# First batch and first run in plain float32 products instead of three split passes

## The chip, the cores and the metric

The kernel runs on one NeuronCore of a Trainium2 chip. The metric is the device time of one execution in microseconds; times are medians over runs, and one further execution is profiled. The engines are named as in the profile: PE (TensorE's matmuls), PEld (its weight loads), DVE (VectorE), ACT (ScalarE), POOL (GpSimd) and SP (SyncE, which issues the DMAs).

## The reference

```python
# q, k, v: (8, 8, 576, 64) float32; w_in (512, 2048), w_out (2048, 512), both float64
k_p = k.reshape(B, H, 72, 8, D).mean(axis=3)          # pooled over 8 positions
v_p = v.reshape(B, H, 72, 8, D).mean(axis=3)
scores = q @ k_p.T / sqrt(D)
attn = softmax(scores)                                # sum + 1e-9
x = (attn @ v_p) -> (B * S, H * D) = (4608, 512)
h = x @ w_in
out = np.maximum(0.01 * h, h) @ w_out                 # (4608, 512) float32
```

The first part is attention against pooled keys and values, the second a two-layer block with a leaky ReLU between the layers. The weights arrive as float64 and are handled as pairs of 32-bit words.

## The kernel before

**Split products.** Most products of the kernel are made in three passes. An operand is held as two float32r tiles: `hi`, its rounded copy (a cast on ACT), and `lo`, the remainder (a subtraction on DVE). A product is then hi x hi + hi x lo + lo x hi, three matmuls that accumulate in one PSUM tile. The score product (L394) alone is a plain float32 matmul.

**Attention.** The eight batches are cut into tiles of 128 or 64 query rows, and neighbouring tiles form pieces of at most 320 rows. The units of a batch have short names: `lk`, `lv` pool k and v; `ku`, `vu` put them in place (`vu` makes `v_hi`, `v_lo` and `v_rem`); `q` transposes a query tile; `sa` makes scores, maximum and exponentials (the sums come with them); `sb` normalises into `at`; `pu` transposes `at` into `pT_hi`, `pT_lo` and `pT_rem`; `au` multiplies by v (L468 to L471) and writes the x tiles `xh` and `xl` of the next layer (L479, L480), or the last 64 rows of batches 0 and 1 into `x_tail`. A tile has two halves g = 0, 1 (four heads each), so `sa31` is tile 3, half 1; a piece too, so `au10` is piece 1, half 0. The last 8 of the 72 pooled positions (`rem`) are held apart.

**Weights.** Both layers are cut into 16 slices f. `stage(f)` has SP load the words of slice f; a conversion consists of a head (two ACT and three DVE instructions, L184 to L190, which make one float32 tile) and a tail (L194 on ACT, L195 on DVE, which make its hi and lo). The steps are issued in a fixed sequence; `c` in the string `FIRST`, and `convert_to(n)` in the main loop, issue the next of them. In the program a conversion's head stands ahead of what follows it; which instruction runs first on ACT, DVE and POOL is decided by a planner from its own costs. PE's order is the program's (manual_schedule).

**Runs.** x is cut into nine chunks of 512 rows. A part is one chunk with one slice f. `m1` computes h for a part (12 matmuls L651 to L653 in two halves, then leaky ReLU L656, cast L659 and subtraction L660 into `gh`, `gl`); `m2` adds its share to the output (12 matmuls L675 to L677), two parts later. Run 0 is chunk 0 with f = 0 to 7, run 1 chunk 1 with all f, run 2 chunk 0 with f = 8 to 15, and so on, one chunk each. The output of run 0 is kept in DRAM as `partial` and added in run 2. The units of the attention that the next chunks need are spread between the halves of m1 and m2: after batch 0's units (the string `FIRST`), run 0 carries the end of batch 0 (`TAIL_STEPS`) and all of batch 1.

**Space.** Weights, the raw k and v of the first batches and other passing tiles share places by tag: `spare(f, i, ...)` is the place of slice f of layer i.

## Time and profile before

| | |
|---|---|
| median of 3 runs | 1011.18 us (1011.02 to 1089.97) |
| profiled execution | 1009.92 us, span of its instructions 1008.1 us |
| granted TensorE clock over the span | 0.978 |
| busy share of PE, PEld | 95%, 78% |
| busy share of DVE, ACT, POOL | 36%, 42%, 18% |
| DMA | 57.44 MB, mean 57 GB/s |

The shares are means over the whole span. The stretch that the change touches is the first 134 us, and there they are quite different; the prediction shows them by stretch. In the rows of the timeline an instruction stands with its start, its duration, engine, line, operation, tiles and count; in brackets the idle time before it and what ended it.

### The profile page before, as it was taken

To read this page: it belongs to the slowest core of one execution; us is meant where nothing else is said; L and a number is where in the kernel's file an instruction comes from. 1 tells how busy PE (TensorE), PEld (TensorE's weight loads), DVE (VectorE), ACT (ScalarE), POOL (GpSimd) and SP (SyncE) were. 2 spreads that over 40 slices of the span, in tenths; PEclk is the share of its full clock that TensorE was granted. 3 is DMA by queue.
4 is the path that set the end of the run, shared out by engine and by line. 5 is a ranking of instruction groups with operands and counts; after the bars stand their busy time and mean duration, and the time that the engine had idled before them with its cause. 6 is when DMAs were issued, how large, how long until landed. Compare 5 with 4: busy or idle time off the path is not lost.

```text
span 1008.1 us, 12812 instructions
## 1 busy us (share of the span) xinstructions
PE 960.3 (95%) x4584; PEld 785.7 (78%) x4584; DVE 366.3 (36%) x890; ACT 427.4 (42%) x1386; POOL 177.7 (18%) x292
## 2 busy tenths in 40 slices
PE   4569999999999999999999999999999999999998
PEld 4457778888887878878888788888887788888886
DVE  5998639223333222232222323232322322231111
ACT  4778657234433333434343425333434334332221
POOL 3602200501036510141013301031100001000000
PEclk8689999999999999999999999999999999999999
DMA  9954311302034301130012202020200020001001
GB/s 241 279 172 133 101 46 44 112 23 69 1 107 115 91 8 44 32 92 12 20 44 58 58 11 63 3 61 1 63 11 11 1 63 1 1 1 42 1 1 42
DMA packets 65006, 57.44 MB, mean 57 GB/s; under 512 B 39856, under 2 KB 48048, under 8 KB 64944
## 3 DMA queue, kind: packets, MB, share of 16 engines
q1 hardware_dynamic: 64944, 56.64, 19.8%
q8 instruction: 36, 0.59, 0.2%
q14 instruction: 26, 0.21, 0.1%
HBM read 46.14 MB, written 10.49 MB: 56 GB/s over the span
## 4 chain that ended last, share of the span: by engine, by line
PE 89%; DVE 4%; ACT 3%; issue 1%; DMA 1%; SPq 0%; POOL 0%; DVEq 0%; ACTq 0%; POOLq 0%
PE ph L651 13%; PE acc L675 13%; PE ph L653 13%; PE ph L652 13%; PE acc L677 13%; PE acc L676 13%; PE pss L394 4%; PE pp L443 2%; PE pq L369 2%; ACT e L404 2%; PE pa L468 1%; PE pa L469 1%; PE pa L471 1%; PE pa L470 1%; DVE w_t L187 1%
## 5 line engine op out<-in xcount | busy, mean ns | idle before, releaser
L651 PE MATMUL ph<-xh,w 128*128 128x512 f32 x576 | 236.2, 410 | 0.0
L675 PE MATMUL acc<-w,gh 128*128 128x512 f32 x576 | 234.7, 408 | 0.0
L653 PE MATMUL ph<-xh,w 128*128 128x512 f32 x576 | 227.2, 394 | 0.0
L652 PE MATMUL ph<-xl,w 128*128 128x512 f32 x576 | 227.0, 394 | 0.0
L677 PE MATMUL acc<-w,gl 128*128 128x512 f32 x576 | 225.7, 392 | 0.0
L676 PE MATMUL acc<-w,gh 128*128 128x512 f32 x576 | 225.5, 392 | 0.0
L656 ACT ACTIVATE ph<-ph 128x512 f32<-128x512 f32 x144 | 84.2, 585 | 275.6 <-PE ph L653 275.4
L660 DVE TENSOR_TENSOR gl<-ph,gh 128x512 fp32r<-128x512 f32 x144 | 99.4, 691 | 264.9 <-ACT gh L659 264.0
L418 POOL TENSOR_TENSOR at<-e,red 128x256 f32<-128x256 f32 (+1 forms) x76 | 47.3, 622 | 561.8 <-DVE red L416 428.0
L404 ACT ACTIVATE e<-pss,red 128x72 f32<-128x72 f32 (+1 forms) x320 | 98.0, 321 | 108.8 <-DVE red L402 107.3
L653 PEld LDWEIGHTS ph<-xh,w 128*128 128x128 f32 x576 | 109.3, 190 | 24.4
L677 PEld LDWEIGHTS acc<-w,gl 128*128 128x128 f32 x576 | 108.4, 188 | 24.1
L651 PEld LDWEIGHTS ph<-xh,w 128*128 128x128 f32 x576 | 109.4, 190 | 22.2 <-issue 1.4
L675 PEld LDWEIGHTS acc<-w,gh 128*128 128x128 f32 x576 | 108.4, 188 | 21.9 <-issue 1.9
L652 PEld LDWEIGHTS ph<-xl,w 128*128 128x128 f32 x576 | 109.6, 190 | 19.4
L676 PEld LDWEIGHTS acc<-w,gh 128*128 128x128 f32 x576 | 108.6, 189 | 19.2
L659 ACT CAST gh<-ph 128x512 fp32r<-128x512 f32 x144 | 85.2, 592 | 3.1
L402 DVE TENSOR_REDUCE red<-pss 128x4 f32<-128x288 f32 (+1 forms) x80 | 36.1, 454 | 99.6 <-PE pss L394 98.5
L404 ACT ACTIVATION_READ_ACCUMULATOR e<-pss,red 128x1 f32 (+1 forms) x320 | 65.8, 206 | 0.0
L394 PEld LDWEIGHTS pss<-kT,qT 128*128 128x128 f32 (+1 forms) x320 | 49.4, 192 | 14.7 <-ACT qT L371 5.0
L394 PE MATMUL pss<-kT,qT 128*128 128x144 f32 (+1 forms) x320 | 55.9, 303 | 4.2 <-ACT qT L371 4.2
L449 DVE TENSOR_TENSOR pT_lo<-pp,pT_hi 128x256 fp32r<-128x256 f32 (+1 forms) x80 | 31.6, 395 | 69.5 <-ACT pT_rem L446 68.7
(90 smaller groups left out, 857.3 us busy)
## 6 DMA issues: line engine op xcount, KB each, us to landing
out_dram<-o SPq DMA_DIRECT2D x35, 256.0 KB, 2.1
q<-in_q_dram SPq DMA_DIRECT2D x32, 256.0 KB, 4.2
w_bits<-in_moe_w_in_dram SPq DMA_DIRECT2D x16, 512.0 KB, 3.6
w_bits<-in_moe_w_out_dram SPq DMA_DIRECT2D x16, 512.0 KB, 3.4
k0raw<-in_k_dram SPq DMA_DIRECT2D x16, 256.0 KB, 3.7
k1raw<-in_k_dram SPq DMA_DIRECT2D x16, 256.0 KB, 4.4
v0raw<-in_v_dram SPq DMA_DIRECT2D x16, 256.0 KB, 4.2
v1raw<-in_v_dram SPq DMA_DIRECT2D x16, 256.0 KB, 5.4
```

The lines of the kernel that those rows point to most:

```text
L394: nc.tensor.matmul(sc[:n, 2 * SP * i : 2 * SP * (i + 1)], qT[:, p, :n], kT[:, p, :, :].rearrange("d i s -> d (i s)"), start=True, stop=True,)
L404: ins = nc.scalar.activation(e[:n, h, :], scv[:n, h, :], AF.Exp, bias=mx[:n, h : h + 1], accum_out=sm[:n, h : h + 1],)
L418: eng.tensor_tensor(at[:n, 0:2, :].rearrange("a i (h s) -> a (i h) s", h=2), e[:n, :, 0:MAIN], sm[:n].unsqueeze(2).broadcast_to([n, 4, MAI ...
L651: nc.tensor.matmul(ph, w[:, 0, ks], xh[kk], start=kk == 0, stop=False)
L652: nc.tensor.matmul(ph, w[:, 0, ks], xl[kk], start=False, stop=False)
L653: nc.tensor.matmul(ph, w[:, 1, ks], xh[kk], start=False, stop=kk == NK - 1)
L656: nc.scalar.activation(ph, ph, AF.Prelu, alpha=0.01)
L659: casts.append(nc.scalar.copy(gh, ph))
L660: nc.vector.tensor_tensor(gl, ph, gh.bitcast(F32), op=ALU.subtract)
L675: nc.tensor.matmul(a, gh[:, r], hi, start=first, stop=False)
L676: nc.tensor.matmul(a, gh[:, r], lo, start=False, stop=False)
L677: nc.tensor.matmul(a, gl[:, r], hi, start=False, stop=last)
```

## The change

For batch 0 the values are kept as one float32 tile `v_first`, and `pT` as one float32 tile (its two main blocks copied by ACT, the remainder block multiplied by the mask `m_lo` on DVE); `au` makes two plain float32 matmuls where there were four. For chunk 0 in run 0, x is one float32 tile (`whole_x`), the weights of slices 0 to 7 stay in the float32 tile that the head makes (`whole_w`), the leaky ReLU writes one float32 tile `g`, and m1 and m2 are one plain float32 matmul per product instead of three split ones. The tails of slices 0 to 7 leave the sequence of steps and are issued when the slice's m2 of run 0 has been issued; `split_first` makes hi and lo of chunk 0's x in the second part of run 1, for run 2. Staging of slice f + 4 is issued behind the head instead of the tail. `FIRST` has 8 conversion steps, all heads, where it had 14 heads and tails, and some tiles lie in other places.

```diff
@@ FIRST
-        "lk ku q0 q1 sa00 sb00 sa01 sb01 lv sa10 sb10 sa11 sb11 q2 sa20 sa21 vu pu00 pu10 c c q3 "
-        "pu01 pu11 c sb20 sb21 au00 sa30 sa31 c au01 c pu20 pu21 sb30 sb31 c c pu30 pu31 c au10 au11 "
-        "c q4 c c / sa40 sa41 sb40 sb41 c c c"
+        "lk ku q0 q1 sa00 sb00 sa01 sb01 lv sa10 sb10 sa11 sb11 q2 sa20 sa21 vu pu00 pu10 c q3 "
+        "pu01 pu11 sb20 sb21 c au00 sa30 sa31 au01 c pu20 pu21 sb30 sb31 c pu30 pu31 c au10 au11 "
+        "q4 c / c sa40 sa41 sb40 sb41 c"
...
+    v_first = wts.tile([P, NK, 2, D], F32, tag="w1_8", name="v_first")
+    nc.gpsimd.memset(v_first, 0.0)
...
+    WHOLE_W = {0: (1, 0), 1: (2, 0), 2: (3, 0), 3: (6, 0), 4: (6, 1), 5: (7, 0), 6: (7, 1)}
+    whole_w = {}
+    def whole_weights(f):
+        if f not in whole_w:
+            shape, name = [P, 2, DM], f"whole{f}"
+            whole_w[f] = (
+                spare(*WHOLE_W[f], shape, F32, name) if f in WHOLE_W
+                else two.tile(shape, F32, tag="raw", name=name)
+            )
+        return whole_w[f]
@@ convert, head
-            ws[i, f] = spare(f, i, [P, 2, DM], F32R, f"w{i}_{f}")
-            t = five.tile([P, DM], I32, tag="o", name=f"w{i}_t{f}")
-            st["w"] = t.bitcast(F32)
+            if f < SPLIT:
+                t = whole_weights(f)[:, i, :]
+                st["w"] = t
+                t = t.bitcast(I32)
+            else:
+                t = five.tile([P, DM], I32, tag="o", name=f"w{i}_t{f}")
+                st["w"] = t.bitcast(F32)
...
+            if i == 1:
+                stage(f + SPARE)
@@ convert, tail
-            w, t = ws[i, f], st["w"]
+            w, t = spare(f, i, [P, 2, DM], F32R, f"w{i}_{f}"), st["w"]
+            ws[i, f] = w
             nc.scalar.copy(w[:, 0, :], t)
             nc.vector.tensor_tensor(w[:, 1, :], t, w[:, 0, :].bitcast(F32), op=ALU.subtract)
-            if i == 1:
-                stage(f + SPARE)
@@ place_v
+            if b == 0:
+                nc.scalar.mul(v_first[r, :, i, :], sums[r], 1.0 / POOL)
+                continue
@@ p_unit
+        if b == 0:
+            anchor["act"] = nc.scalar.copy(pc["hi"][:, :, o : o + n], pp[:, 0:2, :n])
+            nc.vector.tensor_scalar_mul(rem, pp[:, 2, :n], m_lo)
+            return
@@ av_unit
+            if b == 0:
+                vw = v_first[:, p, :, :].rearrange("a i d -> a (i d)")
+                nc.tensor.matmul(pa, vw, pc["hi"][:, i, :w], start=True, stop=False)
+                nc.tensor.matmul(pa, vr.bitcast(F32), pc["rem"][:, :w], start=False, stop=True)
...
-            if m:
+            if m and c == 0:
+                (nc.vector.tensor_copy if i else nc.scalar.copy)(whole_x(p)[:, o : o + m], pa[:, :m])
+            elif m:
...
+    def split_first():
+        for kk, (h, l) in enumerate(zip(*x_parts(0))):
+            nc.scalar.copy(h, whole_x(kk))
+            nc.vector.tensor_tensor(l, whole_x(kk), h.bitcast(F32), op=ALU.subtract)
@@ m1
+        if n == 0:
+            for kk in range(NK):
+                ks = slice(kk * P, (kk + 1) * P)
+                nc.tensor.matmul(
+                    ph, whole_w[f][:, 0, ks], whole_x(kk), start=kk == 0, stop=kk == NK - 1
+                )
+                if kk == 1:
+                    yield
+            g = three.tile([P, CH], F32, tag="gh", name=f"g{nm}")
+            casts.append(nc.scalar.activation(g, ph, AF.Prelu, alpha=0.01))
+            gs[k] = g, None
+            yield
+            return
@@ m2
+            if n == 0:
+                nc.tensor.matmul(a, gh[:, r], whole_w[f][:, 1, :], start=first, stop=last)
@@ steps
+        if f < SPLIT:
+            splits[i, f] = tail
+            continue
@@ main loop
             if n == 0:
-                convert_to(14 + 2.8 * f)
+                convert_to(min(8 + 2 * (f + 1), 2 * SPLIT) + 2 * max(0, f - 3))
             elif n == 1:
-                convert_to(36 + 3 * f)
+                convert_to(2 * SPLIT + 8 + 3 * (f + 1))
+                if f == 1:
+                    split_first()
...
             at += 1
+            for i in range(2):
+                if (i, at - 3) in splits:
+                    splits[i, at - 3]()
```

## The prediction

> **What bounds the kernel now.** First the windows view, cut where the program changes: until 52 us batch 0's attention runs alone, from 52 to 134 us the first run (chunk 0 with f 0 to 7, batch 1's attention beside it), from 134 us the second run. Columns: stretch, length, busy time and instructions of PE, PEld, DVE, ACT and POOL, granted clock, DMA share, GB/s.

> ```profile
> 27.00:52.00 25.00, 12.82 (x64) 10.65 (x64) 25.00 (x51) 16.65 (x53) 16.00 (x18) 0.66 1.00 287
> 52.00:83.00 31.00, 22.72 (x96) 17.71 (x96) 27.84 (x62) 24.91 (x68) 3.85 (x6) 0.83 0.57 171
> 83.00:134.00 51.00, 44.91 (x229) 35.50 (x228) 33.67 (x88) 36.65 (x133) 9.94 (x18) 0.97 0.29 87
> 134.00:220.00 86.00, 86.00 (x381) 71.12 (x380) 42.09 (x79) 40.08 (x76) 13.73 (x18) 1.00 0.21 65
> ```

> From 134 us PE has no idle time, so whatever the change does must show as an earlier or later start of that dense part. DVE is busy 25.00 us of 25 before 52 us and 27.84 of 31 after it; from 83 us PE is nearer to its limit (44.91 of 51) than DVE (33.67). So there are two regimes: DVE sets the pace up to about 83 us, PE after it. The second view is what PE waited for between 27 and 134 us (total, times, longest):

> ```profile
> PE pa L469 <- DVE pT_lo L449: 7.4, 4, 4.5
> PE pp L443 <- DVE at L418: 5.0, 2, 4.3
> PE pp L443 <- DVE x_tail L482: 3.1, 2, 1.8
> PE pp L443 <- POOL at L418: 2.9, 1, 2.9
> PE pq L369 <- ACT e L404: 2.6, 2, 2.1
> PE pq L369 <- DVE kT L330: 2.4, 1, 2.4
> PE pv L357 <- DVE v_rem L360: 0.5, 1, 0.5
> ```

> Three quarters of it end on DVE. Third, PE's timeline with the points where the stretches begin: the first product of the first run (51.94), the fourth m1 (83.12) and the first product of the second run (133.94).

> ```profile
> 51.94 0.50 PE L651 MATMUL ph<-xh,w 128*128 128x512 f32 x1
> ...
> 83.12 0.39 PE L651 MATMUL ph<-xh,w 128*128 128x512 f32 x1
> ...
> 133.94 0.39 PE L651 MATMUL ph<-xh,w 128*128 128x512 f32 x1
> ```

> PE's order is written by hand: 51.94 to 83.12 holds m1 of parts 0 to 2 and m2 of part 0 (16 products of 128x128 by 512), 83.12 to 133.94 holds m1 of 3 to 7 and m2 of 1 to 5 (40), and m2 of parts 6 and 7 (8 products) come after it.

> **The price of a whole product.** A split product is three matmuls. The only plain float32 matmul of before is the score product L394, 144 columns wide.

> ```profile
> L394 PE MATMUL pss<-kT,qT 128*128 128x144 f32 (+1 forms) x320 | 55.9, 303 | 4.2 <-ACT qT L371 4.2
> ...
> 92.57 0.39 PE L653 MATMUL ph<-xh,w 128*128 128x512 f32 x1
> 92.80 0.65 PE L394 MATMUL pss<-kT,qT 128*128 128x144 f32 x4
> 93.19 0.49 PE L651 MATMUL ph<-xh,w 128*128 128x512 f32 x1
> 93.52 0.40 PE L652 MATMUL ph<-xl,w 128*128 128x512 f32 x1
> 93.75 0.40 PE L653 MATMUL ph<-xh,w 128*128 128x512 f32 x1
> ```

> The program calls it 40 tiles x 2 groups x 2 = 160 times and the trace has 320 records: a whole product is two. Start to start a split matmul takes 0.23 us (93.52 to 93.75; 0.228 over longer chains), so three take 0.684. From 92.57 to 93.52 lie one L653, four L394 and one L651: 0.95 - 2 x 0.228 = 0.494, or 0.1235 for 144 columns, 0.858 ns a column. Over 512 columns that is 0.439 a record and **0.878 us a product, 0.194 more than split**. Bounds: if a record's time were mostly fixed, two would cost no less than two split matmuls, 0.456 (0.228 saved); if the columns cost more when long, four split matmuls, 0.912 (0.228 lost). I take 0.878, because the 144-column record has the same mean (303 ns) as the 256-column split matmul beside it (L468, 0.28 to 0.30), as two passes over its columns would give.

> [...]

> **Part A, up to the first product.** DVE never idles between 27 and 44 us, and `at` of tile 3 (L422 at 43.44) is what PE waits for next. What leaves DVE before it:

> ```profile
> 28.86 2.88 DVE L187 SCALAR_TENSOR_TENSOR w_t<-w_bits,w_t 128x512 int32<-128x512 int32 x2
> ...
> 32.79 0.41 DVE L449 TENSOR_TENSOR pT_lo<-pp,pT_hi 128x256 fp32r<-128x256 f32 x1
> 33.13 0.33 DVE L453 SCALAR_TENSOR_TENSOR pT_rem<-pp,marks,pT_rem 128x128 fp32r<-128x128 f32 x1
> ...
> 34.94 0.74 DVE L480 TENSOR_TENSOR xl<-pa,xh 128x256 fp32r<-128x256 f32 x2
> ...
> 35.97 2.55 DVE L195 TENSOR_TENSOR w<-w_t,w 128x512 fp32r<-128x512 f32 x2
> ...
> 43.44 0.40 DVE L422 TENSOR_TENSOR at<-e,red 128x128 f32<-128x128 f32 x1
> ...
> 48.61 0.68 DVE L195 TENSOR_TENSOR w<-w_t,w 128x512 fp32r<-128x512 f32 x1
> ```

> Two weight remainders (2.55; POOL was pooling batch 1 then, and they took twice the 0.68 of 48.61), three pT_lo at 0.34 (1.0), half of four xl (0.7, the other half becomes plain copies): -4.3. The 1.68 us that PE then waits for pT_lo before av of the second piece (46.36, below) become a wait for pT_rem alone, which the change keeps on DVE: -1.1. Against that, av of that piece (16 split matmuls of 256 columns) becomes 16 float32 records. Where PE came out of idleness it ran at half pace:

> ```profile
> 46.36 0.58 PE L469 MATMUL pa<-pT_lo,v_hi 128*128 128x256 f32 x1 [1.68 <-DVE pT_lo L449]
> 46.74 0.42 PE L470 MATMUL pa<-pT_hi,v_lo 128*128 128x256 f32 x1
> 46.96 0.41 PE L471 MATMUL pa<-pT_rem,v_rem 128*128 128x256 f32 x1
> ...
> 95.75 0.28 PE L469 MATMUL pa<-pT_lo,v_hi 128*128 128x256 f32 x1
> 95.86 0.28 PE L470 MATMUL pa<-pT_hi,v_lo 128*128 128x256 f32 x1
> ```

> 0.22 a matmul against 0.11. The av took 16 x 0.213 = 3.4 us; 16 records are 16 x 0.22 = 3.5 at full pace and 7.0 at half. The slow stretch lasted some 3.4 us of steady work (46.36 to 49.8), so half and half: 5.2, +1.8. **A = -4.3 - 1.1 + 1.8 = -3.6.** Bounds: one conversion head fewer also lies ahead (two heads took some 6 us there, their L187 alone 2.88), -8.3; or the planner, which orders DVE by its own costs, puts a head into each freed place and the av runs slowly, +3.6.

> **Part B, 52 to 83 us.** 16 products: +3.1. DVE loses most of the tails and all the gl:

> ```profile
> L195 DVE TENSOR_TENSOR w<-w_t,w 128x512 fp32r<-128x512 f32 x8 | 5.6, 711 | 1.7 <-ACT w L194 1.7
> ...
> L660 DVE TENSOR_TENSOR gl<-ph,gh 128x512 fp32r<-128x512 f32 x3 | 2.1, 686 | 0.0
> ```

> Two of the eight tails come back here (the splits of f = 0 at part 2): 6 x 0.6 + 3 x 0.6 = 5.4 of 27.8 us gone. What PE waits for is late by DVE's backlog: pT_lo 0.9, x_tail 1.3 and 0.2, kT 2.4, v_rem 0.5, in sum 5.3. Heads still come first in the program, so I let half go: -2.7. The POOL wait (2.9) is a chain of max, exponentials and norm; its first link lay 1.1 behind conversion work: -1.0. Then the clock:

> ```profile
> 56.52 0.72 PE L443 MATMUL pp<-ident,at 64*128 64x64 f32 x3 [2.92 <-POOL at L418]
> ...
> 57.77 0.63 PE L652 MATMUL ph<-xl,w 128*128 128x512 f32 x1
> 58.19 0.63 PE L653 MATMUL ph<-xh,w 128*128 128x512 f32 x1
> ...
> 72.58 0.66 PE L369 MATMUL pq<-ident,q 128*128 128x128 f32 x4 [2.44 <-DVE kT L330]
> ...
> 111.21 0.57 PE L369 MATMUL pq<-ident,q 64*128 64x64 f32 x4 [2.08 <-ACT e L404]
> ...
> 129.77 0.52 PE L443 MATMUL pp<-ident,at 128*128 128x128 f32 x3 [1.80 <-DVE x_tail L482]
> ```

> After the gaps of 2.92, 2.44 and 2.08 a stretch at 0.43 a matmul follows; after 1.80 none. In this part about 24 + 6 matmuls lose 0.2 each, 6 us. With the gaps cut below 2 us that loss goes; I take half, -3.0. **B = +3.1 - 2.7 - 1.0 - 3.0 = -3.6**, bounds -8 (all the waits on DVE and the clock) and +1 (only 2 us back).

> [...]

> **Part C, 83 to 134 us.** 40 products: +7.8. Here DVE and ACT aren't the limit; what idle time there is (6.2 us: 2.1, 1.8 and seven under 0.6) is the latency of batch 1's units between two beats of products. A beat grows by 2 x 0.194 = 0.39, which covers the small ones (2.3) and 0.4 of each large one: -3.1. The gl and gh casts that go were hidden by PE. **C = +4.7**, bounds +1.5 (all idle time covered) and +7.8.

> **Part D, after 134 us.** m2 of parts 6 and 7: 8 x 0.194 = **+1.6**, on PE's path. The rest is moved, not removed: the four last tails and split_first (4 casts, 4 subtractions, about 2.4 us of DVE) fall into a stretch where DVE is busy 42 of 86 us, and what reads them runs at least six parts, some 30 us, later; uncovered they would cost their 5 us once. v_first's fill (0.5 us, as for v_hi) lies on an idle POOL ahead of the first pooling. Staging a weight moves from the tail to the head of its conversion, so SP issues it no later; the slots it waits for are freed by the same heads. **The sum: -3.6 - 3.6 + 4.7 + 1.6 = -0.9**, say -1.0, against the profiled execution's 1009.92 us (span 1008.1): 1008.9. The median is 1.3 above that execution, so **1010.2**. No change that a measurement can tell: a comparison of this kernel resolves about 2% (20 us).

> **The rivals.** (1) *PE was the bound all along* (chance 0.2): the products' price stays and the gain doesn't come, because the planner fills DVE's freed time with the next heads, which precede the attention units in the program. Then A is 0, B +1.2 (only the POOL wait's 1.0 and pT_lo's 0.9 come back), C +7.8, D +1.6: +10.6, **1022**. It decides from the point where B's waits on DVE keep their length. For it: PE's 88% from 83 us. Against: three quarters of PE's earlier waits end on DVE. (2) *DVE's backlog was the bound* (0.27): A -6, B -7, C +3, D +1.6: -8.4, **1003**. For it: DVE's full 25 and 27.84 us; A and B take 10 us of work off it. Against: PE's own work is longer by then. (3) *The work is only moved*, and the splits inside the first run take back the room (0.03): before, about 20 heads and 20 tails lie ahead of 134 us; after, 21 heads and 15 tails. That is a difference of 3 us of DVE work, so without the other removals the gain of A and B would be 2 us: **1015**.

> **How the numbers follow.** Forecast (between -5 and +5) 0.5, the rivals as above. From the bounds, the low end takes A -6, B -7, C +2, D +1.6, near -10; the high end A 0, B +1.2, C +7, D +1.6, near +10: **1000 to 1021**. Past 2% either way every term would have to stand at its bound: faster 0.02, slower 0.02, within 2% 0.96.

> **What would show it.** In the profile after: products of the first run as two records each, some 0.44 us apart; the first of them at 48 us (46 to 52); the gaps ahead of pT_rem, kT and x_tail before 83 us at half their length; the second run's first split product at 132 us (124 to 143), and from there a span of 876 us as before plus 1.6. I am wrong if a record of 512 columns isn't near 0.44 us, if PE idles in the second run for a split that is late, or if DVE's order keeps the first product at 52 us.

## The result: 10 to 12 us slower, and the profile after

The changed kernel takes 1021.92 us (median of 4), the kernel before 1011.56 beside it (median of 4): a ratio of 1.0123, 95% interval 1.0101 to 1.0145. (The medians are 10.4 us apart; the ratio, which is taken over fast executions alone, stands for 12.4.) That is within 2%, as forecast, but on the other side of no change, and 0.9 us beyond the range. The profiled execution of after has a span of 1019.1 us, 11.0 over the 1008.1 of before; the parts of the prediction are measured on these two executions.

First the four stretches of the windows view, with the columns as before (length; busy time of PE, PEld, DVE, ACT, POOL; granted clock, DMA share, GB/s):

```profile
27.00:52.00 25.00, 14.19 (x54) 10.46 (x53) 23.95 (x44) 16.50 (x48) 15.83 (x18) 0.72 0.92 256
52.00:83.00 31.00, 20.53 (x69) 11.61 (x69) 30.03 (x64) 23.30 (x57) 2.44 (x4) 0.83 0.71 226
83.00:134.00 51.00, 47.63 (x176) 25.67 (x175) 31.06 (x77) 33.74 (x129) 12.06 (x19) 1.00 0.21 60
134.00:220.00 86.00, 83.31 (x350) 63.72 (x349) 35.55 (x72) 35.77 (x72) 14.78 (x20) 1.00 0.25 71
```

DVE, which was to lose 5.4 us of its 27.84 between 52 and 83 us, is busy for 30.03 of 31. Nothing was freed there: in place of nine heads, eight tails and three `gl` of before it did 13 heads, nine tails and the four subtractions of split_first. Next, what PE waited for between 27 and 150 us:

```profile
PE pp L466 <- DVE at L443: 7.6, 2, 6.8
PE pq L394 <- DVE kT L352: 4.5, 1, 4.5
PE pa L497 <- DVE pT L471: 3.5, 2, 3.1
PE pp L466 <- POOL at L443: 3.0, 1, 3.0
PE pp L466 <- DVE xl L513: 1.9, 1, 1.9
PE pp L466 <- DVE x_tail L515: 1.8, 2, 1.1
PE pv L382 <- DVE v_rem L385: 1.5, 1, 1.5
```

The same producers are late as before (at, kT, the remainder of pT, the POOL norm, x_tail, v_rem), and three are waited for longer: kT 4.5 (2.4), v_rem 1.5 (0.5), the remainder 3.1 (1.68 for pT_lo). The wait for `at` is longer too, 6.8 for 4.3, but it ends earlier (39.28 for 41.92); PE only came to it sooner. The third view is PE's timeline at the points that cut the parts: first product, a whole product at full pace, fourth m1, and run 1's first product (the fourth row; its line is L710).

```profile
54.08 1.98 PE L696 MATMUL ph<-whole_x,whole 128*128 128x512 f32 x4
...
85.08 1.88 PE L736 MATMUL acc<-whole,g 128*128 128x512 f32 x4
86.80 0.65 PE L419 MATMUL pss<-kT,qT 128*128 128x144 f32 x4
...
91.42 1.88 PE L696 MATMUL ph<-whole_x,whole 128*128 128x512 f32 x4
...
144.28 0.39 PE L710 MATMUL ph<-xh,w 128*128 128x512 f32 x1
```

So the first product comes 2.1 us later than before, the fourth m1 8.3, run 1 10.3, and from there to the end it takes 874.8 us (874.2 before). Four records take 1.72 us (85.08 to 86.80): 0.43 each, **0.86 a product**, 0.176 more than split. Last, DVE's timeline: L219 is the second half of a tail, L540 a subtraction of split_first, L211 the end of a head.

```profile
32.40 1.21 DVE L219 TENSOR_TENSOR w<-whole,w 128x512 fp32r<-128x512 f32 x1
...
53.19 0.67 DVE L540 TENSOR_TENSOR xl<-whole_x,xh 128x512 fp32r<-128x512 f32 x1
...
54.73 1.27 DVE L540 TENSOR_TENSOR xl<-whole_x,xh 128x512 fp32r<-128x512 f32 x2
...
57.27 0.67 DVE L540 TENSOR_TENSOR xl<-whole_x,xh 128x512 fp32r<-128x512 f32 x1
...
76.12 0.68 DVE L219 TENSOR_TENSOR w<-whole,w 128x512 fp32r<-128x512 f32 x1
...
77.06 0.68 DVE L211 CUSTOM_DVE_ANT_0 whole<-w_bits,whole 128x1024 uint16<-128x1024 uint16 x1
...
78.10 0.43 DVE L352 TENSOR_SCALAR kT<-pk 64x256 f32<-64x256 f32 x1
```

What the program writes behind run 0 does not run behind it. split_first, written into run 1 (from 144 us), ran at 53 to 58 us; tails ran from 32 us on, 15 of the 16 of slices 0 to 7 ahead of run 1; and a tail and the parts of two heads are the last things ahead of the kT that PE has been waiting for. A deferral in the program's text is none where a planner lays out an engine's order: in this kernel the deferred work took the places that had become free.

### The profile page after: what moved, and what is told of

The parts are those of the page before. It is cut to its first block, busy times and chain, and to the rows that moved or that the text cites. A ratio compares the mean times of both kernels' runs of the same rounds, so it can differ in the third digit from the quotient of the medians.

```text
span 1019.1 us, 12652 instructions
## 1 busy us (share of the span) xinstructions
PE 971.2 (95%) x4520; PEld 772.4 (76%) x4520; DVE 359.8 (35%) x870; ACT 422.6 (41%) x1368; POOL 179.7 (18%) x293
## 4 chain that ended last, share of the span: by engine, by line
PE 82%; DMA 6%; DVE 5%; ACT 4%; SPq 2%; issue 1%; POOL 1%; ACTq 0%; POOLq 0%; DVEq 0%
PE ph L710 12%; PE acc L738 12%; PE ph L712 11%; PE ph L711 11%; PE acc L740 11%; PE acc L739 11%; PE pss L419 3%; PE pp L466 2%; PE acc L736 2%; DMA w_bits<-in_moe_w_out_dram 2%; DMA v1raw<-in_v_dram 1%; PE pq L394 1%; PE ph L696 1%; ACT e L429 1%; SPq L263 1%
## 5 line engine op out<-in xcount | busy, mean ns | idle before, releaser
L710 PE MATMUL ph<-xh,w 128*128 128x512 f32 x544 | 220.9, 406 | 1.1 <-DVE gl L719 1.1
L738 PE MATMUL acc<-w,gh 128*128 128x512 f32 x544 | 220.9, 406 | 0.0
L712 PE MATMUL ph<-xh,w 128*128 128x512 f32 x544 | 212.7, 391 | 0.0
L740 PE MATMUL acc<-w,gl 128*128 128x512 f32 x544 | 212.7, 391 | 0.0
L739 PE MATMUL acc<-w,gh 128*128 128x512 f32 x544 | 212.6, 391 | 0.0
L711 PE MATMUL ph<-xl,w 128*128 128x512 f32 x544 | 212.6, 391 | 0.0
L719 DVE TENSOR_TENSOR gl<-ph,gh 128x512 fp32r<-128x512 f32 x136 | 94.0, 691 | 270.0 <-ACT gh L718 268.8
L443 POOL TENSOR_TENSOR at<-e,red 128x256 f32<-128x256 f32 (+1 forms) x76 | 48.1, 633 | 576.8 <-DVE red L441 401.4
L740 PEld LDWEIGHTS acc<-w,gl 128*128 128x128 f32 x544 | 102.2, 188 | 22.6
L712 PEld LDWEIGHTS ph<-xh,w 128*128 128x128 f32 x544 | 102.2, 188 | 22.6
L710 PEld LDWEIGHTS ph<-xh,w 128*128 128x128 f32 x544 | 102.3, 188 | 22.3 <-DVE gl L719 1.5
L738 PEld LDWEIGHTS acc<-w,gh 128*128 128x128 f32 x544 | 102.2, 188 | 20.5 <-issue 1.4
L711 PEld LDWEIGHTS ph<-xl,w 128*128 128x128 f32 x544 | 102.3, 188 | 18.8 <-issue 0.5
L739 PEld LDWEIGHTS acc<-w,gh 128*128 128x128 f32 x544 | 102.4, 188 | 18.2
L466 PE MATMUL pp<-ident,at 128*128 128x128 f32 (+1 forms) x240 | 40.4, 279 | 14.4 <-DVE at L443 7.6
```

The lines of the kernel that those rows point to most:

```text
L466: nc.tensor.transpose(pp[:, i, :n], at[:n, i, :], ident[:n, :n])
L710: nc.tensor.matmul(ph, w[:, 0, ks], xh[kk], start=kk == 0, stop=False)
L711: nc.tensor.matmul(ph, w[:, 0, ks], xl[kk], start=False, stop=False)
L712: nc.tensor.matmul(ph, w[:, 1, ks], xh[kk], start=False, stop=kk == NK - 1)
L719: nc.vector.tensor_tensor(gl, ph, gh.bitcast(F32), op=ALU.subtract)
L738: nc.tensor.matmul(a, gh[:, r], hi, start=first, stop=False)
```

## The experiments

The theory after the result was: the deferred splits and early heads fill DVE, and their load is what PE waits for (call it load). Its rivals: whole products cost PE 11.3 us (64 x 0.176) and that is the whole story (price); or the order on ACT and DVE, not their load, keeps PE waiting (order). Ratios are to the kernel before on the same chip, with 95% intervals.

**One part alone.** The first kernel is before with only batch 0's attention whole; the second is after with that attention split again.

```
e2: + if b == 0: av_unit, p_unit, place_v as after   (at of tile 2 in slot (11, 1))
e3: - if b == 0: v_first / 2 matmuls   + the 4 split matmuls, pT_lo, v_hi, v_lo
```

> The kernel before, with batch 0's attention alone times v in plain float32; run 0 keeps its split products, order and steps. Theory P: the first product of run 0 starts 2 to 4 us earlier than 51.9 because DVE has less ahead of it, 1007 to 1010. Rival Q: the longer av runs at the low clock and eats that, first product at 52 to 54, 1011 to 1014. Where it is 1009 to 1012 the attention half is neutral.

> The changed kernel, with batch 0's attention in the split passes of before (x is still written as one float32 tile). Theory P: 1020 to 1024, since the loss lies in the products and in the order on DVE, not in the attention. Rival Q (the whole attention costs the 2 us by which the first product came late): 1018 to 1020, first product at 52. If it is above 1024 the whole attention did gain something inside the change.

Attention alone gives 1008.95 us, 0.9982 (0.9972 to 0.9991): 1.8 us gained. That is theory P's time but not its mechanism: in e2's profiled execution (1011.54, the slowest of its ten) the first product comes at 53.91, not earlier than 51.94, so where the gain arises isn't shown. Products alone give 1023.48, 1.0125 (1.0109 to 1.0142): the whole loss. That is 12.6 us by the ratio, and price's 11.3 lies within its interval (11.0 to 14.4), so this run doesn't exclude price.

**Keeping the splits late.** The first kernel ties tails and split_first behind the newest leaky ReLU, so that they can't run early; the second also lets a head follow the newest leaky ReLU instead of the third newest; the third writes each iteration's heads behind its attention units.

```
e1: + with tc.issue_after(casts[-1].ins): splits[i, at - 3]()     (split_first likewise)
e4: e1, and  - BEHIND = 3   + BEHIND = 1
e5: e1, and  convert_to(...) of run 0 moved behind the loop over slots
```

> The changed kernel, with the splits of slices 0 to 7 and split_first made to stand behind the newest leaky ReLU on ACT (the planner had put ten tails and all of split_first ahead of 83 us). Theory P (the planner fills DVE's freed time, so DVE stays the bound until 83 us): the splits leave the full stretch, 5 to 8 us of DVE work, and the time falls from 1022 to 1014 to 1018; the wait of pq for kT before 80 us gets shorter than 4.5. Rival Q (PE's longer products are the whole loss): no change, 1020 to 1024, and the order of DVE is of no account. Rival R (the splits are late for run 1): PE waits in run 1 and the time rises over 1024.

> As the first kernel of this set, and the heads of the conversions stand behind the newest leaky ReLU instead of the third newest, so that they can't run ahead of the attention units. Theory P: the waits for kT, v_rem and x_tail before 90 us shrink to under 4 us in sum (9 in the changed kernel) and the time falls another 2 to 5 us below the first kernel's, 1010 to 1015. Rival Q: no change, 1020 to 1024. Rival R (the heads come too late for m1 and m2): PE waits for whole tiles, over 1022.

> The changed kernel with late splits, and in run 0 the conversion steps of an iteration stand behind its products and attention units in the program instead of ahead of them. With the splits alone late DVE was down to 24 us of 31 between 52 and 83 us and the time stayed at 1022 to 1024, so DVE's load isn't the bound. Theory O (the order is: kT, x_tail and whole_x stand behind heads on ACT and DVE, and ACT waits with a full queue for PE's leaky ReLU): the wait for kT falls from 4.5 us to under 2, that for x_tail under 1, and the time to 1015 to 1020. Rival Q (PE's longer products are all of it): no change, 1021 to 1025. Rival R (heads come too late): over 1025.

Measured: 1023.67 (1.0124, 1.009 to 1.0158), 1024.1 (1.0133, 1.0102 to 1.0165) and 1023.63 (1.0111, 1.0082 to 1.014). The windows of e1 and of e4 for 52 to 83 us, then e1's waits:

```profile
52.00:83.00 31.00, 21.82 (x70) 11.18 (x68) 24.37 (x54) 22.42 (x61) 3.97 (x6) 0.83 0.77 253
```

```profile
52.00:83.00 31.00, 23.58 (x75) 12.55 (x72) 18.19 (x42) 17.43 (x52) 3.97 (x6) 0.83 0.58 179
```

```profile
PE pq L394 <- DVE kT L352: 4.8, 1, 4.8
PE pp L466 <- ACT whole_x L509: 4.6, 1, 4.6
PE pp L466 <- DVE xl L513: 3.2, 1, 3.2
```

DVE's busy time falls from 30.03 to 24.37 and 18.19 of 31, PE's clock stays at 0.83, and no time comes back in sum. From the first product to the fourth m1 e1 takes 38.15 us and e4 36.96, after 37.34: there DVE's load isn't what holds PE. **So load, as the cause, is refuted for that stretch.** Ahead of the first product holding the splits back did help: it comes at 50.96 in e1 and 52.30 in e4, for 54.08 (the 4.6 us for `whole_x` in e1's waits stand where after waits 6.8 for `at`). But from the fourth m1 to run 1 they take 58.26 and 60.09 us, for 52.86; what makes that stretch longer wasn't tried. Why kT is late with an idle DVE shows in e4's timeline of ACT:

```profile
68.70 0.60 ACT L702 ACTIVATE g<-ph 128x512 f32<-128x512 f32 x1 [7.08 <-PE ph L696]
69.20 0.64 ACT L205 ACTIVATE w_bits<-w_bits 128x512 f32<-128x512 f32 x1
69.74 0.66 ACT L206 ACTIVATE w_bits<-w_bits 128x512 int32<-128x512 uint32 x1
70.28 0.67 ACT L205 ACTIVATE w_bits<-w_bits 128x512 f32<-128x512 f32 x1
70.84 0.67 ACT L206 ACTIVATE w_bits<-w_bits 128x512 int32<-128x512 uint32 x1
71.41 0.36 ACT L351 ACTIVATE kT<-pk 64x256 f32<-64x256 f32 x1
```

ACT stands idle for 7.08 us at a leaky ReLU whose products PE hasn't done, then does two heads (which e4 ties behind it), then its half of kT. In e5 the text has the heads behind the units, and PE still waited 4.86 us for kT: ACT's rows there have heads from 57.52 to 67.20 us, broken only by a copy of pT and a leaky ReLU, and kT behind them. They are laid ahead all the same. None of the three came into the range of the theory that it was made for.

**What a microsecond of PE or of DVE is worth.** e9 is before with a fourth pass (low by low) in every product of run 0: 14.6 us more of PE (64 x 0.228), DVE unchanged. e11 leaves out two of before's three passes there: 29.2 us less. e10 is after with one whole product of four: as much PE work as e11, with DVE's work that of after.

```
e9:  + if n == 0: nc.tensor.matmul(ph, w[:, 1, ks], xl[kk], ...)   + a <- gl, lo
e10: + if kk == f % NK: nc.tensor.matmul(...)                      + if t != f % NT: continue
e11: + if n == 0: nc.tensor.matmul(ph, w[:, 0, ks], xh[kk], ...)   + a <- gh, hi alone
```

> The kernel before, with a fourth pass (lo x lo) in every product of run 0: 64 matmuls of 0.228 us more on PE, 14.6 us, 12.8 of them ahead of the second run; DVE, ACT and SP have the same work. Theory S (serial: PE's waits lie between neighbours in its order, so products never cover them and every microsecond of product counts): +12 to +15, 1023 to 1026. Rival D (DVE's backlog is the bound up to 83 us and products there are covered): 16 products of that stretch cost nothing, +8 to +11, 1018 to 1021. Rival H (half is covered everywhere): under +8.

> The changed kernel with one of the four whole products in each m1 and m2 of run 0 (the other three are left out), 0.86 us a part and layer instead of 3.44; DVE and ACT keep all work. Beside it runs the kernel before with one pass instead of three, 0.91. PE's product work is so about equal and what differs is DVE's and ACT's. Theory S alone: 56 and 8 products lose 0.86 x 48 = 41 us, 981, if no new wait comes. Theory D (whole products relieve DVE, the relief is only hidden by PE's price): this kernel ends 4 us or more below the other. Rival (no relief, since the planner fills the room): within 2 us of it or above it.

> The kernel before with one pass (hi x hi) in each product of run 0; the two passes with lo are left out, all casts, subtractions and tails stay. PE loses 128 x 0.228 = 29 us. Theory S: 982 to 986. Theory D: up to 83 us DVE holds it back, only the 40 products after that and the 8 behind count, -22, 988 to 992.

Measured: e9 1020.42 (1.0086, 1.0056 to 1.0116), e10 1003.92 (0.9923, 0.9895 to 0.9951), e11 1002.4 (0.9918, 0.9895 to 0.9942). Their stretches from 27 to 83 us, in the same order (of e10 and e11 the second alone):

```profile
27.00:52.00 25.00, 11.82 (x55) 9.90 (x55) 25.00 (x49) 16.66 (x54) 15.60 (x18) 0.62 0.98 280
52.00:83.00 31.00, 27.05 (x108) 21.11 (x108) 26.86 (x60) 22.38 (x64) 2.94 (x5) 0.76 0.54 169
```

```profile
52.00:83.00 31.00, 14.20 (x56) 9.89 (x55) 29.87 (x64) 23.46 (x57) 2.53 (x4) 0.61 0.68 224
```

```profile
52.00:83.00 31.00, 19.93 (x71) 14.74 (x70) 29.22 (x66) 24.91 (x69) 2.92 (x5) 0.56 0.59 186
```

Added PE work reaches the end at 9.3 of 14.6 us, 0.64 (0.39 to 0.80 by the interval); removed work at 8.7 of 29.2, 0.30 (neither of e11's two theories had so little). e9's time is in theory D's range, but not for D's reason: in its profiled execution the 16 passes up to the fourth m1 cost 3.3 of their 3.6 us and the 40 after it 4.9 of 9.1, so the products are not covered where DVE is full. And e10 and e11, with much the same PE work in products (16 x 0.86 = 13.8 and 64 x 0.228 = 14.6), end at the same time to within some 4 us by their intervals: **all that the change takes from DVE is worth nothing** that these runs can tell, in the order that after has. In both DVE is full between 52 and 83 us (29.87, 29.22): whatever room is made, heads move up into it. By 0.64 the whole products should cost 7.2 us (4.4 to 9.0), not price's 11.3, and the change, with e2's -1.8, +5.4. It cost 10.4 to 12.4, so 5 to 7 us (3 to 10 by e9's interval) are not explained by PE's work.

**The order.** e12 holds heads of slices 4 to 7 on ACT behind batch 1's kT. e13 (on e1) lets heads and steps go one at a time, each behind one attention unit of batch 1 on ACT (kT, a qT, an exponential). e6 and e14 are e2 with e5's and with e13's order.

```
e12: + if 4 <= f < SPLIT: after = anchor["kT"]           and  convert_to(...) of run 0 only from f = 2 on
e13: e1, and  + after = anchor.get("now") or after          (head, on ACT)
     + if n == 0 and "unit" in anchor:                      (behind each unit)
     +     anchor["now"] = anchor.pop("unit"); convert_to(min(stepped + 1, 24))
     + convert_to(2 * f + 2)                                (run 0, in place of after's)
e6:  e2, and  convert_to(15 + 2.8 * f) behind the loop over slots
e14: e2, and  the lines of e13 (cap 35, and 4 * f + 5 for 2 * f + 2)
```

> The changed kernel, with the heads of slices 4 to 7 held on ACT behind batch 1's kT copies, so that these no longer stand behind them. The wait of pq for kT (4.5 us) falls under 1.5 if the heads ahead of it make it. Theory O (a wait taken from PE's order is gone for good): 1017 to 1020. Rival (the waits only move on, as the kernels with late splits had it): 1021 to 1025. If kT's wait stays over 3, the heads that are left ahead of it make it, or POOL's sums.

> The changed kernel with late splits, and the heads of slices 4 to 7 and the steps after them one at a time: each stands on ACT behind one unit of batch 1 (kT, each qT, each group of exponentials), so that no burst of heads stands ahead of a unit. Theory O (the excess over PE's price is the order: bursts of heads ahead of single units): PE's waits between the first product and 83 us fall from 9.9 to under 5 us, 1015 to 1019. Rival S (PE's price and the fixed chains are all of it): waits fall but run 0 stays near 90 us, 1020 to 1024. Over 1025 the heads came too late for m1.

> The kernel before with whole attention for batch 0 (1009.0 beside 1010.4), and the conversion steps of run 0 behind its units in the program. Theory O: waits for kT, x_tail and v_rem fall from 5.2 us to under 3, 1004 to 1008. Rival (in split run 0 the tails are needed at once, so they can't wait): 1009 to 1014.

> The kernel before with whole attention for batch 0 (1009.0) and the conversion steps of run 0 one at a time behind the units of batch 1 in the same way. Theory O: waits after the first product fall from 12.8 to under 9 us, 1003 to 1007. Rival: in split run 0 the tails are due at once and come too late, 1009 to 1014.

e12 gave 1024.96 (1.0138, 1.0114 to 1.0162), as its rival had it. Two rows of its PE timeline say why:

```profile
70.92 0.66 PE L398 MATMUL pq<-ident,q 128*128 128x128 f32 x4 [0.77 <-DVE kT L354]
...
79.43 1.33 PE L423 MATMUL pss<-kT,qT 128*128 128x144 f32 x4 [6.13 <-ACT qT L400]
```

kT is no longer late (0.77 for 4.5), and the heads that were held, now all ready at once, stand ahead of the next unit, qT, and make that wait 6.13. The wait is moved on, not removed. e13 gave 1018.73, 1.0073 (1.0058 to 1.0088), in theory O's range and 5 us under e1, and its interval ends below e1's; no other edit that keeps all of the change's whole products does that. Its windows line and two of its waits:

```profile
52.00:83.00 31.00, 26.63 (x105) 15.00 (x104) 20.47 (x48) 20.27 (x69) 7.44 (x10) 1.00 0.47 148
```

```profile
PE pp L473 <- DVE xl L520: 3.7, 1, 3.7
...
PE pv L385 <- DVE v_rem L388: 1.3, 1, 1.3
```

kT's wait is 0.77, PE does 26.63 us of work in 31 (e1 21.82) at a clock of 1.00 (0.83), and run 1 starts at 139.29 us (e1 147.37). What is left of the loss, 7.4 (5.9 to 8.9), is 2 us over the 5.4 that PE's price and e2 give, and the intervals overlap (2.6 to 7.2). e13 changes the heads' pace with their places, so these two aren't told apart. With split products the same orders gain nothing over e2: e6 1009.01 (0.998, 0.9961 to 1.0), e14 1009.47 (0.9988, 0.9972 to 1.0005), both where their rivals had them and not at theory O's 1003 to 1008.

How much of this is gained, and where, shows when one profiled execution of each is cut at the same events (us):

| kernel | first product at | to the fourth m1 | from there to run 1 | from run 1 to the end |
|---|---|---|---|---|
| before | 51.94 | 31.18 | 50.82 | 874.2 |
| after | 54.08 | 37.34 | 52.86 | 874.8 |
| e1 | 50.96 | 38.15 | 58.26 | 875.4 |
| e13 | 50.79 | 25.00 | 63.50 | 877.2 |
| e14 | 51.84 | 26.30 | 57.34 | 874.0 |

e13's order takes 12.3 us out of after's second column, which is then shorter than before's, and 10.6 of them come back in the third, where PE idles for 9.5 us and its clock is 0.92. So in e13 order and pace set PE's waits up to the fourth m1, but most of what they free there is waited for later, as in e12. Of the 2.6 us by which this execution of e13 is shorter than after's, 3.3 lie ahead of the first product and 1.7 between it and run 1, and 2.4 are lost behind. e13 and e14 also compare whole with split products in much the same order: 8.6 us by the ratios, which is what whole products cost there (7.2, 4.4 to 9.0, by e9). Between after and e2, in the order of after and of before, it is 14.3.

**Two further runs.** e7 puts 80 unused transposes into the two long waits ahead of the first product, to keep PE's clock up there. e8 takes only slices 0 to 2 whole in run 0.

```
e7: + 55 x nc.tensor.transpose(pp[:, 0, :], ident, ident)   (tile 3)   + 25 x ... (piece 1)
e8: + NW = 3;  m1, m2, head and steps: n == 0 and f < NW;   split_first ahead of part 3
```

> The changed kernel with 80 unused transposes on PE, 55 ahead of pu30 and 25 ahead of au10, where PE waits 6.8 and 3.1 us; their results are overwritten. Theory K (PE's clock falls in these waits and the whole av pays twice): av of piece 1 at 0.22 us a record instead of 0.43, the first product at 50 to 52 us instead of 54.1, 1018 to 1020. Rival (the av's clock isn't what sets the first product, DVE's rem is): first product at 53 to 55, 1021 to 1023. Rival (the fillers outlast the waits): first product over 55, over 1023.

> The changed kernel, with only slices 0 to 2 of run 0 in whole products; slices 3 to 7 are converted, split and multiplied in three passes as before (x is split ahead of m1 of part 3). Theory Q (the price of PE's products counts where PE is the limit, from 83 us): 40 of the 64 products get 0.18 us shorter, -7.0, 1013 to 1017. Theory O alone (order decides, products don't): 1019 to 1024. If DVE's backlog was what the change relieved, the tails and gl that come back cost as much again: 1020 to 1026.

e7: 1025.4 (1.0139, 1.0117 to 1.0161), the third rival's figure. Its clock from 27 to 52 us is 0.89 (after 0.72) and both waits are nearly gone, yet the first product comes at 55.64, behind a new wait of 3.06 for ACT's qT. The av runs at full pace (0.22 us a record, 0.43 in after) and PE is at q's transposes at 50.02 us (52.03 in after), so the slow clock did cost 2 us there; but ACT now does a tail's cast and two casts of split_first ahead of qT, and they take the gain away. What holds the first product in this run is again an order, this time on ACT.

```profile
27.00:52.00 25.00, 21.59 (x135) 19.07 (x134) 23.91 (x43) 15.78 (x45) 14.85 (x18) 0.89 0.90 249
```

e8: 1014.47 (1.0038, 1.0021 to 1.0056), in theory Q's range. 24 products x 0.176 = 4.2 us of PE; measured +3.8 over before. Against after, e8 takes 40 x 0.176 = 7.0 us from PE and gives DVE the tails and `gl` of slices 3 to 7 back, and it is 7.4 us faster (8.6 by the ratios): the products' price is real, and DVE's relief doesn't pay for it. Of the three numbers of whole products that were run (0 in e2, 24, 64) the larger is the slower each time.

## Why the prediction was wrong, point by point

The step that failed is **the relief in parts A and B**: that 4.3 and 5.4 us less of DVE work, taken from a DVE that is always busy, come back as shorter waits of PE. In after the relief did not take place (DVE 30.03 for 27.84 between 52 and 83 us, PE's idle time in B 11.5 us for 8.3), and where it did, in e1 and e4, B stayed as long (38.15 and 36.96 us, after 37.34). e10 against e11, at much the same PE work, and e8 agree. The windows view again, cut this time at the three events (first product, fourth m1, run 1), first of before, then of after:

```profile
51.94:83.12 31.18, 22.90 (x96) 17.86 (x96) 28.02 (x64) 25.03 (x69) 3.85 (x6) 0.84 0.57 172
83.12:133.94 50.82, 44.73 (x228) 35.35 (x227) 33.50 (x86) 36.53 (x133) 9.94 (x18) 0.97 0.29 87
```

```profile
54.08:91.42 37.34, 25.85 (x81) 14.10 (x80) 33.17 (x72) 26.94 (x74) 4.06 (x7) 0.86 0.71 221
91.42:144.28 52.86, 49.37 (x188) 26.91 (x187) 30.72 (x78) 33.67 (x122) 11.80 (x18) 1.00 0.09 25
```

- *Price of a whole product*: forecast 0.878, measured 0.860. For 64 products +11.3 instead of +12.4. Right. The trace stays below four times the split matmul's 0.228 (0.912).
- *A, forecast -3.6, measured +2.1.* at of tile 3 did come earlier (transposes at 41.28, 43.57 before): -2.3 of -4.3. The wait for the remainder grew by 1.5 where it was to shrink by 1.1. The av behind that wait took 2.0 more at a slow clock (0.50 until 51.2 us), as forecast (1.8), and the transposes and the first two records ahead of it another 1.0. But this point can't be read finer than some 2 to 3 us: in e9 and e11, which change nothing ahead of the first product, it came at 54.20 and 55.02 instead of 51.94.
- *B, forecast -3.6, measured +6.2.* Products +2.8 (forecast 3.1). PE's idle time grew from 8.3 us (31.18 - 22.90) to 11.5, +3.2, where -3.7 was forecast; the clock gave little back (0.84 to 0.86) where 3.0 us were; that term rested on a reading that before's own rows contradict (last section). I had counted work as gone that was only written elsewhere: DVE did tails, split_first and more heads in the place.
- *C, forecast +4.7, measured +2.0.* Products +7.0 (forecast 7.8); idle time 6.1 to 3.5, -2.6 (forecast -3.1); PE's busy time rose by 4.6 alone, 2.4 less than the products. What I left out is the clock, 0.97 to 1.00: before has 3.4 us at half pace here (granted clock 0.50 from 111.4 to 114.8) and after none, which is 1.7 of the 2.4; the rest isn't worked out. Mechanism right, size off.
- *D, forecast +1.6, measured +0.7.* Products +1.4. Of the splits that I had costed here as hidden, 15 of 16 tails and all of split_first ran ahead of run 1; the cost I named for them uncovered never came. (DVE's 35.55 for 42.09 between 134 and 220 us has another source: eight heads for twelve and 13 `gl` for 16; the tails are twelve in both.)
- *Rivals.* The first gave the time (1022), with its mechanism in the place where it was put: the planner fills freed time with heads, and the waits on DVE in B keep their length. Its terms are off (A +2.1 for 0, B +6.2 for +1.2, C +2.0 for +7.8), so the agreement of the sum is in part luck; that PE alone was the bound is not so, by e9, e11 and e13. The second, DVE's backlog as the bound, is what e1 and e4 disprove for B, and e8 for the whole. The third, splits inside run 0, did happen, but undoing it (e1) gained nothing in sum.
- *What would show it*: records 0.44 apart, yes; first product at 46 to 52, no; gaps halved, no; run 1 at 132 (124 to 143), no, 144.28; a constant remainder, yes within 0.9.

In sum, by the ratios: -1.2 for whole attention with e13's order (e14), +8.6 for whole products in that order (e13 against e14), +5.0 for after's order in place of e13's: the 12.4 of the change. The first two are measured as such. That the last 5 us are order and pace is argued, not shown: e13 changes both at once, in the profiled executions its gain over after is 2.6 us, and 3.3 us of gain lie ahead of the first product, a point that moves by as much between kernels with the same work ahead of it. Open, too, is why the same orders gain nothing with split products: the planner orders by its own costs, and what it assumes for a float32 matmul was not tried.

## What to carry to other kernels

A busy engine is not a bound: ask what it is busy with just ahead of the instruction that is waited for, and whether that work has to stand there. Work that a program defers can come back early where a planner may place it, and idle room that an edit makes is filled, as here; if it is to stay away, tie it to an instruction of the engine's own order, one piece behind one unit, and then look where the waits have gone, for they may only have moved. And before pricing a relief, price both engines by runs that change one of them alone: here 1 us of PE cost 0.6 us when added and gave 0.3 back when taken away, and 1 us of DVE was worth nothing as long as the order stayed.

## What the runs showed of the hardware

I had tied half pace to the length of the one gap ahead of it, with none after gaps under 2 us. Before's own rows say otherwise: behind gaps of 0.89 and 1.25 us the split matmuls take 0.43 us each, as at half pace.

```profile
61.05 0.30 PE L469 MATMUL pa<-pT_lo,v_hi 128*128 128x64 f32 x1 [0.89 <-DVE pT_lo L449]
...
63.26 0.37 PE L443 MATMUL pp<-ident,at 64*128 64x64 f32 x3 [1.25 <-DVE x_tail L482]
...
64.13 0.63 PE L652 MATMUL ph<-xl,w 128*128 128x512 f32 x1
64.56 0.63 PE L653 MATMUL ph<-xh,w 128*128 128x512 f32 x1
```

So does after's timeline:

```profile
59.03 0.63 PE L466 MATMUL pp<-ident,at 64*128 64x64 f32 x3 [2.96 <-POOL at L443]
59.59 1.98 PE L696 MATMUL ph<-whole_x,whole 128*128 128x512 f32 x4
62.52 0.43 PE L496 MATMUL pa<-pT,v_first 128*128 128x64 f32 x2 [0.95 <-ACT pT L470]
63.28 0.43 PE L497 MATMUL pa<-pT,v_rem 128*128 128x64 f32 x2 [0.33 <-DVE pT L471]
...
65.31 0.56 PE L466 MATMUL pp<-ident,at 64*128 64x64 f32 x3 [1.15 <-DVE x_tail L515]
65.80 3.78 PE L696 MATMUL ph<-whole_x,whole 128*128 128x512 f32 x4
```
